# Larger slot distances in a slot-scheduled attention and MLP kernel: loads, q/k transposes, result stores

## The chip, the cores and the metric

One core of a Trainium2 chip. The metric is the device time of one execution, in microseconds (us). A profiled execution shows a span about 1.7 us shorter than the time of its run; numbers from a trace are compared with numbers from a trace only. The profiled execution of the kernel before took 338.71 us, 2 us less than the median of 340.72.

Engines: PE multiplies matrices, DVE is the vector engine, ACT the activation engine, POOL issues the casting loads, SP issues the transposes by DMA and the stores. "SPq" in a profile line is SP's queue.

## The reference, cut to what matters

```python
# B, H, S, D = 4, 8, 768, 64; chunks of 32 keys
k_min, k_max = min and max of k over each chunk
ub = sum_d max(q * k_min, q * k_max)             # a bound per query and chunk
top_chunks = the 6 chunks of largest ub, causal
attn = softmax(where(mask, q @ k.T / sqrt(D), -1e9)) @ v
x = attn, heads merged                           # 3072 x 512
out = softplus(x @ w_in) @ w_out                 # 512 -> 2048 -> 512
```

## The kernel before

The work is cut into 12 blocks of 256 query rows (block n), and time into "slots": one slot is one pair of score tiles (two score matmuls and their exponential on ACT, so 192 slots and 192 score exps). A block has 8, 16 or 24 slots. Other work is hung onto slot numbers: `at(slot, generator)` runs a piece of the preparation of a later block, `later` is a list of things that become due at a slot, and each slot also advances the MLP of earlier blocks by one step.

```python
    def turn_dma(nm, n, pool):                   # q or k transposed by DMA, issued on SP
        x_sb = loaded.pop((nm, n))
        xt = pool.tile([128, NT, NP, 128], BF16, name=nm + "t")
        nc.sync.dma_start_transpose(out=..., in_=...)
        turned[nm, n] = xt

    def prep_block(n):                           # all of this on DVE, except the two marked
        kt = turned.pop(("k", n))
        ...
        for t in range(NT):
            nc.vector.tensor_reduce(kx[:, 0, t], kc, axis=AX.X, op=ALU.max)   # kxf <- kt
            nc.vector.tensor_reduce(kx[:, 1, t], kc, axis=AX.X, op=ALU.min)
            yield
        put_extremes(...)                        # bd <- kxf
        qt = turned.pop(("q", n))
        nc.vector.tensor_scalar_max(qpos, qt, 0.0)
        yield
        ... qneg, qa
        for t in range(NT):
            bounds(...)                          # PE: ub <- bd, qpos, qneg; DVE: ub_sb, 8 largest
            choose(...)                          # mraw
            yield
        nc.sync.dma_start_transpose(out=mt, in_=mraw)     # SP
        ... ka, kb <- kt
        put_mask(n, mt, 0, 2)                    # qa, qt <- mt

    def ot_step(n, g, o_sb):                     # attention result turned to x, on SP
        nc.sync.dma_start_transpose(out=X[n]..., in_=o_sb...)
        if g == 1:
            ready[n] = clock[0] + 4              # the MLP of block n may start

    def y_gen(n):
        for u in range(NT):
            y = ps_y.tile(...)                   # ONE buffer in PSUM
            for f in range(KFF):
                nc.tensor.matmul(y, g[...], w_out_sb[...])
                ...
                        nc.vector.tensor_copy(y_sb, y)
                        nc.sync.dma_start(out=out[r0:r0 + 128, :], in_=y_sb)
```

SP and POOL issue in the order in which the code emits their work, from start to end. DVE, PE and ACT do so only for block 0; from block 1 on, the framework's scheduler picks their order when the program is built, from its own estimate of when each operand will be there. Once built, DVE works through its list in order, and an instruction that waits holds up all behind it: all 615 DVE instructions ran in the order of the built list.

The softmax here doesn't subtract the row's maximum and nothing guards it: scores larger than these inputs give would overflow.

## Time and profile before

| | kernel before |
|---|---|
| time, median of 3 runs | 340.72 us |
| span of the profiled run | 337.0 us |
| first score exp of block 2 | 79.7 us |
| last score exp | 307.2 us |
| from there to the end ("tail", MLP only) | 29.8 us |

I call the time between these two score exps the stream: 79.7 to 307.2 us, 227.5 us. What comes before it is the start, what comes after it the tail. The page of the kernel before, its span, PE's busy share, granted clock in tenths over 40 slices, and the chain that ended last by engine:

```profile
span 337.0 us, 6388 instructions
...
PE 261.4 (78%) x2411; PEld 185.2 (55%) x2440; DVE 168.5 (50%) x615; ACT 197.2 (59%) x350; POOL 115.7 (34%) x191
...
PEclk9999999856997999969999979789999799999999
...
PE 43%; DVE 23%; DMA 20%; ACT 4%; SPq 3%; POOL 3%; issue 2%; ACTq 0%
```

No engine is full, PE is the nearest, and its clock dips again and again. The list of waits of the same kernel (who waited for whom: us in total, times, longest):

```profile
DVE kxf L289 <- DMA kt<-k_sb: 30.1, 9, 7.8
...
PE y L415 <- DVE y_sb L420: 17.2, 7, 6.0
...
PE ub L201 <- DVE qpos L298: 10.1, 5, 2.9
...
DVE qa L279 <- DMA mt<-mraw_115: 8.3, 5, 2.7
...
DVE qa L279 <- DMA mt<-mraw_114: 7.7, 4, 3.3
```

How such waits reach PE is seen in the timeline of the kernel before around its longest stop in the stream (start, duration, engine, line, operation, output<-input; in brackets the idle time before and what ended it):

```profile
204.22 1.19 SPq L381 DMA_TRANSPOSE x<-o_sb  x1
...
205.51 1.25 SPq L166 DMA_TRANSPOSE kt<-k_sb  x1
...
212.00 0.69 DVE L289 TENSOR_REDUCE kxf<-kt 128x16 bf16<-128x512 bf16 x1 [7.81 <-DMA kt<-k_sb]
...
216.85 0.68 DVE L420 COPY y_sb<-y 128x512 f32<-128x512 f32 x1
...
217.58 1.86 PE L415 MATMUL y<-w_out_sb,g 128*128 128x512 bf16 x4 [6.02 <-DVE y_sb L420]
```

SP issues kt only at 205.5 us; DVE has kxf next in its list and stands for 7.8 us; the y_sb copy behind it is late; y has one PSUM buffer, so PE stands for 6.0 us. Then PE runs at half clock, as the table of windows shows (window and its length, then busy us of PE, PEld (PE's weight loads), DVE, ACT and POOL with the number of instructions, then clock, DMA share, GB/s):

```profile
211.50:217.60 6.10, 0.08 (x3) 0.02 (x1) 5.51 (x16) 0.70 (x2) 2.16 (x3) 0.77 1.11 86
217.60:221.30 3.70, 3.70 (x14) 1.99 (x14) 0.99 (x3) 0.60 (x1) 0.00 (x0) 0.50 0.37 106
221.30:224.00 2.70, 2.70 (x28) 1.96 (x27) 0.00 (x0) 2.39 (x5) 1.24 (x2) 0.95 0.00 0
```

In the stream the PE stops of 0.4 us and more add up to 24.6 us, and the clock stands at half for 25.9 us (about 13 us lost, if PE had work all that time).

The row of a DMA on its issuing engine is only its issue: kt takes 1.25 us on SP and lands a median of 4.7 us after its issue began. The Trainium skill ("Perfetto Trace Analysis", section "Per-instruction lifecycle") says that on DMAs the entire data movement falls outside the profiled window; this trace agrees.

### The profile page before, as it was taken

To read this page: it belongs to the slowest core of one execution; us is meant where nothing else is said; L and a number is where in the kernel's file an instruction comes from. 1 tells how busy PE (TensorE), PEld (TensorE's weight loads), DVE (VectorE), ACT (ScalarE), POOL (GpSimd) and SP (SyncE) were. 2 spreads that over 40 slices of the span, in tenths; PEclk is the share of its full clock that TensorE was granted. 3 is DMA by queue.
4 is the path that set the end of the run, shared out by engine and by line. 5 is a ranking of instruction groups with operands and counts; after the bars stand their busy time and mean duration, and the time that the engine had idled before them with its cause. 6 is when DMAs were issued, how large, how long until landed. Compare 5 with 4: busy or idle time off the path is not lost.

```text
span 337.0 us, 6388 instructions
## 1 busy us (share of the span) xinstructions
PE 261.4 (78%) x2411; PEld 185.2 (55%) x2440; DVE 168.5 (50%) x615; ACT 197.2 (59%) x350; POOL 115.7 (34%) x191
## 2 busy tenths in 40 slices
PE   1234579428978879589899699299898799999994
PEld 0122447124665567457575587167665677776561
DVE  5877700287687565616854652737454932112001
ACT  3333359104893479547774869168764798886180
POOL 8334796422542633412445404213431110100000
PEclk9999999856997999969999979789999799999999
DMA  9929999996995992946966949937946211011101
GB/s 173 206 43 162 106 182 178 148 84 127 86 153 43 131 135 52 109 64 108 82 79 114 170 46 81 107 35 125 108 67 111 65 31 49 33 39 40 47 33 62
DMA packets 121374, 32.14 MB, mean 95 GB/s; under 512 B 115200, under 2 KB 117760, under 8 KB 121344
## 3 DMA queue, kind: packets, MB, share of 16 engines
q0 software_dynamic: 67168, 12.33, 48.9%
q1 hardware_dynamic: 51024, 18.62, 28.3%
q10 hardware_dynamic: 3152, 0.79, 1.4%
q8 instruction: 19, 0.31, 0.4%
q14 instruction: 11, 0.09, 0.1%
HBM read 27.26 MB, written 6.29 MB: 100 GB/s over the span
## 4 chain that ended last, share of the span: by engine, by line
PE 43%; DVE 23%; DMA 20%; ACT 4%; SPq 3%; POOL 3%; issue 2%; ACTq 0%
PE y L415 19%; PE hp L402 13%; DMA kt<-k_sb 10%; PE o_ps L363 4%; PE s_ps L338 3%; DVE y_sb L420 3%; DMA q_sb<-in_q_dram 3%; DMA two<-in_k_dram 3%; DVE kxf L290 3%; DVE kxf L289 3%; PE s_ps L340 2%; DMA x<-o_sb 2%; DVE bd_112 L191 2%; DMA qt<-q_sb 2%; DVE qpos L298 1%
## 5 line engine op out<-in xcount | busy, mean ns | idle before, releaser
L342 ACT ACTIVATE pt<-s_ps 128x512 bf16<-128x512 f32 (+1 forms) x192 | 103.3, 550 | 85.3 <-PE s_ps L340 85.2
L402 PE MATMUL hp<-x,w_in_sb 128*128 128x256 bf16 x768 | 107.1, 283 | 11.9 <-DMA x<-o_sb 11.1
L415 PE MATMUL y<-w_out_sb,g 128*128 128x512 bf16 x355 | 96.9, 395 | 19.1 <-DVE y_sb L420 17.2
L346 POOL TENSOR_SCALAR_AFFINE_SELECT pt<-pt 128x256 bf16<-128x256 bf16 x96 | 39.7, 415 | 174.6 <-ACT pt L342 174.4
L402 PEld LDWEIGHTS <-w_in_sb 128*128 128x128 bf16 x768 | 74.6, 101 | 23.8 <-issue 11.8
L404 ACT ACTIVATE e_sb<-hp 128x512 f32<-128x512 f32 x96 | 57.8, 605 | 31.7 <-PE hp L402 31.6
L415 PEld LDWEIGHTS <-g 128*128 128x128 bf16 x384 | 35.8, 100 | 48.7 <-issue 22.8
L406 ACT ACTIVATE g<-e_sb 128x1024 bf16<-128x1024 f32 x48 | 51.2, 1067 | 0.2
L420 DVE COPY y_sb<-y 128x512 f32<-128x512 f32 x24 | 16.5, 688 | 38.2 <-PE y L415 38.0
L363 PEld LDWEIGHTS <-pt 128*128 128x128 bf16 x672 | 32.0, 102 | 4.8 <-issue 0.6
L369 DVE RECIPROCAL rec<-o_ps 128x4 f32<-128x4 f32 x48 | 8.6, 179 | 48.8 <-PE o_ps L363 48.4
L289 DVE TENSOR_REDUCE kxf<-kt 128x16 bf16<-128x512 bf16 x20 | 13.6, 680 | 30.2 <-DMA kt<-k_sb 30.1
L373 DVE TENSOR_TENSOR o_sb<-o_ps,rec 128x256 bf16<-128x256 f32 x48 | 20.2, 422 | 1.4 <-DVE rec L369 0.3
L113 POOL DMA_DIRECT2D k_sb<-in_k_dram x20 | 17.8, 894 | 8.4 <-DMA kt<-k_sb 4.8
L363 PE MATMUL o_ps<-v_106,pt 128*128 128x65 bf16 x336 | 20.2, 202 | 0.1
L113 POOL DMA_DIRECT2D q_sb<-in_q_dram x20 | 18.0, 904 | 1.9 <-DMA qt<-q_sb 1.3
L363 PE MATMUL o_ps<-v_107,pt 128*128 128x65 bf16 x336 | 16.3, 195 | 0.8 <-DVE o_sb L373 0.8
L203 DVE TENSOR_TENSOR ub_sb<-ub,cmask 128x192 f32<-128x192 f32 x20 | 7.0, 352 | 16.7 <-PE ub L202 16.7
L338 PE MATMUL s_ps<-qa,ka_108 96*128 96x256 bf16 x48 | 14.8, 309 | 0.6 <-ACT pt L342 0.4
L338 PE MATMUL s_ps<-qt,kb_110 128*128 128x256 bf16 x48 | 14.9, 311 | 0.4 <-ACT pt L342 0.3
L279 DVE COPY qa<-mt 32x512 bf16<-32x512 bf16 x20 | 6.7, 333 | 16.4 <-DMA mt<-mraw_115 8.3
L338 PE MATMUL s_ps<-qt,kb_111 128*128 128x256 bf16 x48 | 13.5, 281 | 0.0
(147 smaller groups left out, 309.2 us busy)
## 6 DMA issues: line engine op xcount, KB each, us to landing
out_dram<-y_sb SPq DMA_DIRECT2D x24, 256.0 KB, 2.2
k_sb<-in_k_dram POOLq DMA_DIRECT2D x20, 128.0 KB, 4.7
q_sb<-in_q_dram POOLq DMA_DIRECT2D x20, 128.0 KB, 5.3
w_in_sb<-in_moe_w_in_dram POOLq DMA_DIRECT2D x4, 512.0 KB, 5.6
w_out_sb<-in_moe_w_out_dram POOLq DMA_DIRECT2D x4, 512.0 KB, 7.7
v_107<-in_v_dram POOLq DMA_DIRECT2D x12, 128.0 KB, 4.9
v_106<-in_v_dram POOLq DMA_DIRECT2D x10, 128.0 KB, 4.2
two<-in_k_dram SPq DMA_DIRECT2D x6, 128.0 KB, 6.2
```

The source lines that it names most:

```text
L113: nc.gpsimd.dma_start(out=xb[:, t], in_=rows(nm, n, t))
L289: nc.vector.tensor_reduce(kx[:, 0, t], kc, axis=AX.X, op=ALU.max)
L338: nc.tensor.matmul(s_ps[:, 0:QB], kk[0:nr, p, j * 128:(j + 1) * 128], qq[0:nr, :, p, :], start=True, stop=True)
L342: nc.scalar.activation(pt[:, h, j:j + 2].rearrange("k j c -> k (j c)")[:, 0:w], s_ps[:, 0:w], ACT.Exp, scale=scale)
L346: nc.gpsimd.affine_select(out=diag, in_=diag, compare_op=ALU.is_ge, fill=0.0, base=0, channel_multiplier=-1, pattern=[[0, 2], [1, 128]])
L363: nc.tensor.matmul(o_ps[:, u, h], pt[:, h, j, c0:c0 + 128], V[b % 2][:, j, 2 * p + h, :], start=(j == 0), stop=(j == t0 + u))
L373: nc.vector.tensor_tensor(o_sb[:, :, p % 2], o_ps[:, :, :, 0:D], rec.to_broadcast([128, NT, 2, D]), op=ALU.mult)
L402: nc.tensor.matmul(hp[:, fi], w_in_sb[:, dt, ft * 128:(ft + 1) * 128], X[n][:, dt // 2, :, dt % 2, :], start=(dt == 0), stop=(dt == KDM - 1))
L404: nc.scalar.activation(e_sb[:, f2 * 2:f2 * 2 + 2], hp, ACT.Exp)
L406: nc.scalar.activation(g[:, f4 * 4:(f4 + 1) * 4], e_sb, ACT.Ln, bias=1.0)
L415: nc.tensor.matmul(y, g[:, f, u * 128:(u + 1) * 128], w_out_sb[:, f, :], start=(f == 0), stop=(f == KFF - 1))
L420: nc.vector.tensor_copy(y_sb, y)
```

## The change

The intent is to take waits away by distance: data asked for earlier, and stores issued only when their data is surely there, so that the in-order SP queue is not held up.

```diff
-            later.append((clock[0] + 2, 0.0, ot_step, (n, p // 2, O.pop((n, p // 2)))))
+            later.append((clock[0] + 4, 0.0, ot_step, (n, p // 2, O.pop((n, p // 2)))))
...
-            ready[n] = clock[0] + 4
+            ready[n] = clock[0] + 6
...
-                        nc.sync.dma_start(out=out[r0:r0 + 128, :], in_=y_sb)
+                        if clock[0] == NEVER:
+                            store(r0, y_sb)
+                        else:
+                            later.append((clock[0] + 3, 0.0, store, (r0, y_sb)))
...
-        if n == 2:
-            base = 17
+        base = {2: 17, 3: 32}.get(n, base)
...
-            at(base - PER - 6, later_loads(n))
+            at(base - PER - 10, later_loads(n))
...
-        at(base - (4 if n > 2 else 1), turns)
-        at(base - (3 if n > 2 else 1), turns)
+        at(base - (12 if n > 2 else 1), turns)
+        at(base - (9 if n > 2 else 1), turns)
```

So there are three parts: loads and q/k transposes earlier, with block 3's preparation moved from slot 26 to 32 ("turns"), stores later ("stores"), x transposes and the MLP start later ("x delay").

More of the change, by code (lines that the diff above doesn't have):

```diff
@@ L407, in h_gen, with store @@
                 yield
+    def store(r0, y_sb):
+        nc.sync.dma_start(out=out[r0:r0 + 128, :], in_=y_sb)
     def y_gen(n):
```

## The prediction

> **What bounds it now.** No engine is full: the page gives PE 78% of 337.0 us, ACT 59%, DVE 50%. PE is the limit wherever nothing stalls: in the table of windows it is busy 25.8 of 26 us at 284-310, clock 1.00. Elsewhere it stops. From 76 to 310 us it is busy 204.9 of 234 us. The timeline of PE names the stops over 0.5 us: y matmuls waiting for the y_sb copy on DVE (4.5, 1.6, 6.0, 0.8 us), ub matmuls waiting for qpos on DVE (2.9, 2.1, 2.8, 1.9), one x transpose (1.4); about 24 us. After most of the longer ones the clock reads 0.50 to 0.59 for some 3.7 us (144.3-148.0: 0.50), about 1.8 us lost each, 8 us in all. The Trainium skill ("TensorE: Matmul & The Clock Gate", Part 1) says an idle window of about 3.4 us halves the clock; this trace agrees roughly (also after 1.9 us).
>
> DVE is late because it is in order and sits on kxf until the kt transpose lands: 30.1 us in 9 waits (list of waits), 9.9% of the chain. kt is late because the SP queue is in order too: it stands behind result stores and mask transposes whose data DVE has not made (64 and 44 us of SP waits for y_sb), then takes 4.7 us to land.
>
> **What changes.** No arithmetic, no bytes. In SP's built order kt of the next block moves ahead of the mask transpose mt; qt comes right behind mt; stores fall back three slots. Loads go 4 slots earlier. x transposes come 2 slots later and the MLP starts 4 slots later: by counting slots, 4 MLP steps (about 0.9 us each) move into the tail, roughly neutral because PE is full there.
>
> **How much is won.** Not all 32 us. DVE and PE order is chosen by the scheduler, and the built DVE order shows it also hoists kxf and qpos: often right behind what releases their transpose. So DVE still stops on kt (two in three blocks of a period, 4 to 6 us), and newly on qt: mt and qt are issued back to back (1.2 us each), mt lands in 2.4, qt in 5.1, with 1.2 us of mask copies between, so some 2.5 us a block. But qpos is then ready long before its ub matmuls, so the ub stops go, and the y stops shrink. Walking one period of three blocks (72 us) with trace durations I get PE stops of about 1, 2, and 3 to 4 us (y and o_ps matmuls waiting for DVE evacuations), about 6.5 us plus perhaps 2 us of slow clock, against 12 and 3.5 now: 7 us a period, 3.3 periods in the stream. The start to 79 us is bound by loads and stays, within 2 us.
>
> **Prediction: 319 us** (-21), range 308 to 333. Faster by over 2%: 0.86; within 2%: 0.12; slower: 0.02.
>
> **Signs.** Stops of ub for qpos nearly gone; y_sb stops under 3 us each; clock over 76-310 us above 0.95; kxf waits for kt from 30 to about 20 us; new qpos waits for qt of 10 to 18 us; SP waits on y_sb well under 64 us; tail after the last score 3 to 4 us longer; PE busy time about unchanged or less (warmer clock).
>
> **What would make it wrong.** If the hoisted kxf/qpos block o_sb and y_sb evacuations longer than I walked (each 6 us stop passing wholly to PE), the gain falls to a few us. If transposes land faster in an emptier queue, DVE never stops and 305 is possible. If block 5's earlier loads slow the crowded start, up to 4 us come back.

## The result, and the profile after

The changed kernel takes 330.86 us (330.64 to 331.73, 3 runs) against 340.72: ratio 0.9729, 95% interval 0.9679 to 0.9779. A ratio here is the mean time of one kernel's runs over that of the other's runs of the same rounds, so not quite the ratio of the quoted medians. Executions over 1.5% slower than the fastest of the same kernel are left out of the means. The direction was right and the time lay in the range, but the gain was 9.9 us where 21.7 were forecast (340.72 to 319).

The page after:

```profile
span 329.1 us, 6389 instructions
...
PE 256.9 (78%) x2409; PEld 183.7 (56%) x2440; DVE 163.4 (50%) x615; ACT 197.0 (60%) x350; POOL 117.2 (36%) x191
...
PEclk9999999965897899999979999999799999999998
...
PE 33%; DMA 27%; DVE 25%; ACT 6%; issue 3%; SPq 3%; POOL 2%; ACTq 0%; POOLq 0%
```

PE's matmul share is 78% in both, though the time differs by 2.7%. The Trainium skill ("Perfetto Trace Analysis", section "Identifying the Most-Contended Engine") calls matmul busy % no good measure of how near PE is to its roofline, and proposes MFU (the share of peak FLOP/s) and the busy share of LDWEIGHTS (PE's weight loads). No run here computes MFU, and the share of weight loads moved only from 55% to 56%, so neither share by itself shows the gain.

The list of waits after:

```profile
DVE kxf L289 <- DMA kt<-k_sb: 34.3, 8, 7.2
...
DVE qa L279 <- DMA mt<-mraw_115: 13.8, 5, 3.9
PE y L418 <- DVE y_sb L423: 11.4, 7, 3.6
...
DVE qa L279 <- DMA mt<-mraw_114: 10.6, 4, 3.3
...
PE ub L201 <- DVE qpos L298: 7.4, 1, 7.4
PE ub L201 <- DVE ub_sb L203: 6.9, 3, 5.6
```

The transposes stand 9 to 12 slots ahead in the code instead of 3 or 4, and DVE waits for kt not less but more: 34.3 us, where it was 30.1. (The one wait of ub for qpos, 7.4 us, lies at 70 us, before the stream.) The timeline after, around the longest such wait of DVE in the stream:

```profile
224.17 0.42 DVE L373 TENSOR_TENSOR o_sb<-o_ps,rec 128x256 bf16<-128x256 f32 x1
...
224.62 1.19 SPq L381 DMA_TRANSPOSE x<-o_sb  x1
...
225.91 1.25 SPq L166 DMA_TRANSPOSE kt<-k_sb  x1
...
231.79 0.69 DVE L289 TENSOR_REDUCE kxf<-kt 128x16 bf16<-128x512 bf16 x1 [7.20 <-DMA kt<-k_sb]
...
235.05 0.69 DVE L423 COPY y_sb<-y 128x512 f32<-128x512 f32 x1
...
235.79 1.44 PE L418 MATMUL y<-w_out_sb,g 128*128 128x512 bf16 x3 [3.55 <-DVE y_sb L423]
```

The same picture as before: DVE goes from the o_sb evacuation straight to kxf, and SP can issue kt only after the x transpose that this o_sb releases. The built order of DVE says why; this is the place of one such kxf, that of block 8, in the lists of the changed kernel (engine, number in its list without waits and branches, line, operation, operands; from the built program, not from the profile):

```
DVE 363  L373 TensorTensor  o_sb_2052<-o_ps_2129,rec_2161
DVE 364  L289 TensorReduce  kxf_2559<-kt_2318
SP   51  L381 DmaTransposeAnt  x_2221<-o_sb_2052
SP   52  L166 DmaTransposeAnt  kt_2318<-k_sb_2010
```

The code emits this kxf twelve slots after its kt; the scheduler has pulled it up to right behind the instruction that sets the transpose off. The distance in the code is twelve slots, that in DVE's list is nothing.

How far each kernel has come at the start of a given score exp (us from the start of the span, from the timeline of ACT):

| score exp number | before | after | difference |
|---|---|---|---|
| 25th (block 2) | 79.7 | 79.3 | -0.4 |
| 57th (block 4) | 114.2 | 117.4 | +3.2 |
| 105th (block 7) | 184.3 | 181.7 | -2.6 |
| 153rd (block 10) | 257.0 | 249.3 | -7.7 |
| 192nd, the last | 307.2 | 296.5 | -10.7 |
| end of span | 337.0 | 329.1 | -7.9 |

The first lap is 3.6 us slower (from -0.4 to +3.2), the others gain 5.8, 5.1 and 3.0 us, and 2.8 us are given back in the tail, which grows from 29.8 to 32.7 us (rounded from the trace).

### The profile page after: what moved, and what is told of

It is laid out like the page before. It is cut to its first block, busy times and chain, and to the rows that moved or that the text cites. A ratio compares the mean times of both kernels' runs of the same rounds, so it can differ in the third digit from the quotient of the medians.

```text
span 329.1 us, 6389 instructions
## 1 busy us (share of the span) xinstructions
PE 256.9 (78%) x2409; PEld 183.7 (56%) x2440; DVE 163.4 (50%) x615; ACT 197.0 (60%) x350; POOL 117.2 (36%) x191
## 4 chain that ended last, share of the span: by engine, by line
PE 33%; DMA 27%; DVE 25%; ACT 6%; issue 3%; SPq 3%; POOL 2%; ACTq 0%; POOLq 0%
PE y L418 16%; DMA kt<-k_sb 12%; PE hp L402 9%; DMA k_sb<-in_k_dram 5%; DMA two<-in_k_dram 3%; PE s_ps L338 3%; DVE y_sb L423 3%; DMA mt<-mraw_115 3%; DVE kxf L290 2%; DMA mt<-mraw_114 2%; PE s_ps L340 2%; PE o_ps L363 2%; DVE kxf L289 2%; DVE o_sb L373 2%; ACT g L406 2%
## 5 line engine op out<-in xcount | busy, mean ns | idle before, releaser
L418 PE MATMUL y<-w_out_sb,g 128*128 128x512 bf16 x353 | 93.5, 386 | 13.6 <-DVE y_sb L423 11.4
L346 POOL TENSOR_SCALAR_AFFINE_SELECT pt<-pt 128x256 bf16<-128x256 bf16 x96 | 40.5, 423 | 161.5 <-ACT pt L342 161.4
L402 PEld LDWEIGHTS <-w_in_sb 128*128 128x128 bf16 x768 | 73.8, 100 | 17.1 <-issue 5.1
L404 ACT ACTIVATE e_sb<-hp 128x512 f32<-128x512 f32 x96 | 58.5, 613 | 24.4 <-PE hp L402 24.1
L418 PEld LDWEIGHTS <-g 128*128 128x128 bf16 x384 | 35.1, 98 | 41.6 <-issue 14.7
L423 DVE COPY y_sb<-y 128x512 f32<-128x512 f32 x24 | 16.5, 687 | 42.6 <-PE y L418 42.5
L289 DVE TENSOR_REDUCE kxf<-kt 128x16 bf16<-128x512 bf16 x20 | 13.6, 678 | 34.3 <-DMA kt<-k_sb 34.3
L363 PE MATMUL o_ps<-v_106,pt 128*128 128x65 bf16 x336 | 19.5, 201 | 1.7 <-DVE o_sb L373 1.6
L113 POOL DMA_DIRECT2D q_sb<-in_q_dram x20 | 18.7, 937 | 2.5 <-DMA qt<-q_sb 1.3
L363 PE MATMUL o_ps<-v_107,pt 128*128 128x65 bf16 x336 | 15.9, 193 | 0.8 <-DVE o_sb L373 0.8
L338 PE MATMUL s_ps<-qa,ka_108 96*128 96x256 bf16 x48 | 15.5, 324 | 0.5 <-ACT pt L342 0.5
L338 PE MATMUL s_ps<-qt,kb_110 128*128 128x256 bf16 x48 | 14.7, 306 | 0.5 <-ACT pt L342 0.3
L340 PE MATMUL s_ps<-qa,ka_108 96*128 96x128 bf16 (+1 forms) x48 | 13.9, 289 | 0.0
L338 PE MATMUL s_ps<-qa,ka_109 96*128 96x256 bf16 x48 | 13.5, 281 | 0.0
```

Of the source, the lines that this page charges most:

```text
L113: nc.gpsimd.dma_start(out=xb[:, t], in_=rows(nm, n, t))
L338: nc.tensor.matmul(s_ps[:, 0:QB], kk[0:nr, p, j * 128:(j + 1) * 128], qq[0:nr, :, p, :], start=True, stop=True)
L340: nc.tensor.matmul(s_ps[:, QB:w], kk[0:nr, p, (j + 1) * 128:(j + 2) * 128], qq[0:nr, 1 if last else 0:, p, :], start=True, stop=True)
L346: nc.gpsimd.affine_select(out=diag, in_=diag, compare_op=ALU.is_ge, fill=0.0, base=0, channel_multiplier=-1, pattern=[[0, 2], [1, 128]])
L363: nc.tensor.matmul(o_ps[:, u, h], pt[:, h, j, c0:c0 + 128], V[b % 2][:, j, 2 * p + h, :], start=(j == 0), stop=(j == t0 + u))
L402: nc.tensor.matmul(hp[:, fi], w_in_sb[:, dt, ft * 128:(ft + 1) * 128], X[n][:, dt // 2, :, dt % 2, :], start=(dt == 0), stop=(dt == KDM - 1))
```

## The experiments

Theory: what was won is small because the scheduler hoists the DVE readers of the transposes (kxf, qpos, and their companions) up to the transposes, so the new distance never reaches DVE. Rival one: the transposes themselves come too late, in the in-order SP queue or the crowded DMA, and the order of DVE does not matter. Rival two: another part of the change (stores, x delay) carries the gain, or spoils it. All experiments gave correct results. Each batch ran beside the kernel before on one chip (7 runs of it, medians 339.03, 341.00 and 340.06 us, one slow run in the last). The x delay alone was not run.

The table holds all runs; times are medians of the fast executions, of two only for early_as_before (their mean); "stops" are PE's idle stretches of 0.4 us or more within the stream (25th to 192nd score exp), "half" the time within it at a clock of 0.5, both from the profiled run. "kxf" is DVE's total wait of kxf for kt from the list of waits.

| run | time, us | ratio (95%) | stream | tail | stops | half | kxf |
|---|---|---|---|---|---|---|---|
| before | 340.72 | 1 | 227.5 | 29.8 | 24.6 | 25.9 | 30.1 |
| after | 330.86 | 0.973 (0.968 to 0.978) | 217.2 | 32.7 | 18.9 | 19.3 | 34.3 |
| turn_only | 331.29 | 0.973 (0.963 to 0.982) | 220.3 | 29.8 | 24.9 | 10.2 | 42.4 |
| store_only | 328.93 | 0.970 (0.961 to 0.978) | 217.6 | 29.4 | 17.5 | 19.2 | 35.1 |
| no_x_delay | 329.41 | 0.972 (0.965 to 0.980) | 218.7 | 29.4 | 22.0 | 10.2 | 40.9 |
| early_as_before | 331.51 | 0.974 (0.967 to 0.981) | 217.6 | 32.6 | 20.2 | 18.7 | 33.2 |
| dve_order | 313.26 | 0.924 (0.919 to 0.929) | 200.7 | 32.6 | 6.8 | 12.2 | 10.6 |
| before_dve_order | 316.60 | 0.934 (0.928 to 0.939) | 207.0 | 29.8 | 8.3 | 15.9 | 18.8 |
| pin_turned | 314.33 | 0.925 (0.919 to 0.930) | 199.8 | 32.7 | 7.9 | 3.6 | 6.1 |
| before_pin_turned | 320.60 | 0.942 (0.937 to 0.947) | 208.3 | 29.8 | 11.9 | 11.4 | 13.4 |
| dve_order_turn_only | 309.53 | 0.911 (0.901 to 0.922) | 201.1 | 29.8 | 3.9 | 9.3 | 10.5 |
| dve_order_no_x_delay | 307.28 | 0.908 (0.901 to 0.915) | 197.5 | 29.4 | 2.9 | 4.0 | 9.8 |

### dve_order and before_dve_order: DVE in the order of the code

```diff
-    consts(1)
-    run_block(1, 0.8)
-    ...
+    with tc.manual_schedule(engines={ET.DVE}):
+        consts(1)
+        run_block(1, 0.8)
+        ...
```

Only the order of DVE is fixed; PE and ACT stay with the scheduler, which moves some of their work in answer (588 of PE's 4880 instructions changed place in the built list, by 2.5 places in the mean over all). Once on the changed kernel, once on the kernel before.

> Changed kernel, with DVE kept in program order from block 1 on, so that kxf and qpos stand where their slot puts them, 12 and 11 slots behind their transposes. If the scheduler's hoisting eats the new distance (my theory): waits of kxf for kt fall from 34 us to under 10 us, PE stops over 0.5 us between 76 and 310 us from about 24 us to under 12 us, time 316 to 325 us. If the transposes themselves come late on the in-order SP queue or the crowded DMA (rival): the waits stay above 25 us and the time at 327 to 334 us.

> Kernel before, with DVE in program order in the same way. Theory: the distance of 4 slots is too short whatever the order, kxf waits for kt stay at 15 to 30 us, time 332 to 342 us. Rival (the order of DVE alone is worth the gain, the distances nothing): as fast as the changed kernel with DVE in order, within 3 us.

The changed kernel drops to 313.26 us, further than the theory's 316 to 325; the waits for kt fall to 10.6 us, a hair above the 10 it allowed. The waits for kt and for y_sb in dve_order, from its list of waits:

```profile
DVE kxf L289 <- DMA kt<-k_sb: 10.6, 1, 10.6
...
PE y L418 <- DVE y_sb L423: 1.1, 2, 0.8
```

The one wait for kt left is that of block 2, at the start, whose transpose is issued one slot ahead in all versions. PE stops in the stream fall to 6.8 us. Rival one falls: SP issues the same transposes in the same order (its sequence in the two traces is the same), and the waits are gone.

The second run did not do what I expected. The kernel before, with DVE in the order of the code, takes 316.60 us, where I expected 332 to 342; kxf still waits 18.8 us (10.3 of it at the start), inside my 15 to 30. The other 8.5 us lie in the stream, and part of them reaches PE: four ub stops for qpos, 6.6 us together, come 4 to 5 us behind such waits. So 4 slots are a little short, but my belief that they are too short whatever the order is wrong in size: the two kernels with DVE in order differ by 3.3 us (the rival had said within 3), the two with the scheduler's order by 9.9, and the order alone is worth 22 us to the kernel before, more than twice the whole change.

### pin_turned and before_pin_turned: only the readers of the transposes held

Program order moves all of DVE's work. To see whether the readers of the transposes alone matter, those were queued behind the evacuation that was emitted last before their slot (order of issue only, no wait on data):

```diff
+        evac[0] = nc.vector.tensor_tensor(o_sb[:, :, p % 2], ...)     # likewise at y_sb
...
+            with tc.issue_after(evac[0].ins):
                 nc.vector.tensor_reduce(kx[:, 0, t], kc, axis=AX.X, op=ALU.max)
                 nc.vector.tensor_reduce(kx[:, 1, t], kc, axis=AX.X, op=ALU.min)
...                      # the same around qpos, around qneg and qa, around ka, around kb
```

> Changed kernel with only the DVE readers of the q and k transposes (kxf, qpos, qneg, qa, ka, kb copies) held behind the evacuation emitted last before their slot; all other DVE order is the scheduler's. Theory (hoisting of these readers is what eats the distance): 311 to 317 us like the run with DVE in order, kxf waits for kt under 15 us. Rival (DVE in order won by other moves, of masks, bounds or y_sb): 322 to 331 us.

> Kernel before with the same hold. It got 316.6 us with all of DVE in order. Theory (the readers of the transposes alone): 314 to 322 us, with 15 to 25 us of kxf waits, since 4 slots are short. Rival (other moves): 328 to 340 us.

Both came out where the theory put them: 314.33 and 320.60 us. The line of kt in pin_turned, and that of PE:

```profile
DVE kxf L291 <- DMA kt<-k_sb: 6.1, 1, 6.1
...
PE y L424 <- DVE y_sb L429: 5.5, 5, 3.0
```

Holding back six kinds of DVE instruction in five places, and nothing else, gives within about 1 us what DVE in full program order gives the changed kernel, and in the kernel before most of it (ratio 0.942 against 0.934). The scheduler was free to move other work when they were held, but in before_pin_turned it did not: PE's weight loads, ACT, POOL and SP run through the same sequence in its trace as in that of the kernel before, and the built lists of PE agree too. Only DVE's order differs, and the time falls by 20 us. The hoisting of these readers, as a group, is shown to be the cost, in both kernels; which of the six counts most was not tried. Where they are held, the whole change is worth 6 us (320.60 to 314.33); in before_pin_turned kxf still waits 13.4 us for kt, less than the 15 to 25 us I expected:

```profile
DVE kxf L291 <- DMA kt<-k_sb: 13.4, 5, 7.0
```

### turn_only, store_only, no_x_delay: the parts of the change

turn_only leaves out the later stores and the x delay; store_only has only the stores; no_x_delay leaves out only this:

```diff
-            later.append((clock[0] + 4, 0.0, ot_step, ...))
+            later.append((clock[0] + 2, 0.0, ot_step, ...))
-            ready[n] = clock[0] + 6
+            ready[n] = clock[0] + 4
```

> Only loads and q/k transposes earlier; stores and x transposes as before. Theory: this part carries the gain of the stream and costs no tail: 327 to 332 us. Rival (the later stores clear the SP queue, and that is the gain): 335 to 341 us.

> Kernel before with only the stores three slots behind. Theory: kt still stands behind the mask transpose on SP, its readers are hoisted, so 335 to 341 us. Rival (clearing SP of stores that wait for y_sb is the gain): 328 to 334 us.

> Changed kernel with x transposes and the MLP start at the old 2 and 4 slots. Theory: the later MLP start costs about 3 us of tail and some of the early stop of PE for x at 78 us (5.8 us), so 325 to 329 us, tail after the last score exp back from 32.6 to about 30 us. Rival (the x delay is what lets kt pass on SP): 331 to 336 us.

The turns alone give 331.29 us, as expected. The stores alone give 328.93 us, and here the rival was right: I expected no gain. Each of the two yields about the whole gain, and together they yield no more; why they do not add up is open. The traces show different ways. With the stores alone the ub stops for qpos shrink (9.8 to 2.4 us in the stream), the long y stops stay. With the turns alone the sum of stops does not change (24.6 and 24.9 us) and kxf waits most of all (42.4 us), but the time at half clock falls from 25.9 to 10.2 us: it has one stop over 3 us in the stream, the kernel before has two, of 4.5 and 6.0 us. That many small stops cost less clock than a few long ones is read from these two traces alone; which stop halves the clock I can not say in each case.

Taking the x delay out gave 329.41 us, a hair above my 325 to 329, and the same ratio as the whole change (0.972 and 0.973). The tail is back to 29.4 us, and the stream is longer by 1.5 us. So with the scheduler's order the delay does no measurable good or harm.

### early_as_before: block 3 as before

The slow first lap (25th to 57th exp) suggested that block 3's move did harm: its preparation at slot 32 and its kt ahead of block 2's mask.

```diff
-        base = {2: 17, 3: 32}.get(n, base)
+        if n == 2:
+            base = 17
...                      # and for n = 3 the transposes 4 and 3 slots ahead
```

> Changed kernel, with block 3 as before (preparation at slot 26, its transposes 4 and 3 slots ahead). Theory: the move of block 3's kt ahead of the mask of block 2, and of its preparation to slot 32, makes the start slow, so the 56th score exp comes back from 117.4 to about 114.5 us and the total is 326 to 329 us. Rival (the earlier loads or the later x do it): 56th exp stays at 116 to 118 us, total 330 to 333 us.

That theory fell. The 57th exp (the expectation counts from zero and calls it the 56th) came at 115.6 us, between what the two expected, the last exp at 296.5 us as in the changed kernel, and two executions took 330.85 and 332.17 us, as the rival said. The trace of the changed kernel says better what slows the lap: at 104.2 us PE stands 5.6 us for ub_sb, because DVE waited for block 3's mask (2.4 us) and then, in front of ub_sb, for the kt of block 5:

```profile
95.03 1.45 SPq L166 DMA_TRANSPOSE kt<-k_sb  x1
...
96.07 0.28 DVE L279 COPY qa<-mt 32x512 bf16<-32x512 bf16 x1 [2.37 <-DMA mt<-mraw_115]
...
100.67 0.69 DVE L289 TENSOR_REDUCE kxf<-kt 128x16 bf16<-128x512 bf16 x1 [2.69 <-DMA kt<-k_sb]
...
103.78 0.34 DVE L203 TENSOR_TENSOR ub_sb<-ub,cmask 128x192 f32<-128x192 f32 x1
...
104.17 0.20 PE L201 MATMUL ub<-bd_113,qpos 128*128 128x48 bf16 x1 [5.63 <-DVE ub_sb L203]
```

The same stop is in turn_only (5.9 us) and no_x_delay (5.8 us), and it is in neither store_only nor pin_turned. So it goes both without the earlier turns and without the hoisted reader.

### dve_order_no_x_delay and dve_order_turn_only: what beats both

These combine DVE in order with the whole change less the x delay, and with the turns alone.

> Changed kernel, DVE in program order, x transposes and MLP start at the old 2 and 4 slots. Theory (PE is full both in the stream and in the tail, so 4 MLP steps cost the same in either): within 2 us of 313 us, the tail after the last score exp shorter by about 3 us and the stream longer by as much. Rival (the shorter tail is a gain of its own): 309 to 311 us.

> Only loads and q/k transposes earlier, DVE in program order. Theory (with the readers in place the transposes' distance is what is left of the change): 312 to 315 us, like the whole change with DVE in order. Rival (the stores give the last 3 us): 316 to 318 us, like the kernel before with DVE in order.

The first is the fastest of all, 307.28 us, 9.2% under the kernel before and 6 us under dve_order; I had expected no difference, and even the rival's 309 to 311 was too high. Its page shows what PE looks like without stops (busy tenths and clock over the 40 slices):

```profile
PE   0333369914799879999999999999999999999984
...
PEclk9999996975599999999999999999999999999999
```

Where the 6 us come from: in dve_order the x transposes come later and the MLP starts later, so PE has less to do in the gap around 75 to 85 us. There it stands 4.8 us for the mask copies of block 2 and 2.3 us for an x; without the delay these are 1.7 and 2.0 us. First two lines dve_order, last two dve_order_no_x_delay:

```profile
77.73 0.37 PE L338 MATMUL s_ps<-qa,ka 96*128 96x256 bf16 x1 [4.77 <-DVE qa L279]
...
83.98 0.58 PE L402 MATMUL hp<-x,w_in_sb 128*128 128x256 bf16 x2 [2.30 <-DMA x<-o_sb]
...
75.28 1.01 PE L402 MATMUL hp<-x,w_in_sb 128*128 128x256 bf16 x4 [2.04 <-DMA x<-o_sb]
...
78.00 0.37 PE L338 MATMUL s_ps<-qa,ka 96*128 96x256 bf16 x1 [1.71 <-DVE qa L279]
```

The half-clock time falls from 12.2 to 4.0 us, and at the 57th exp the kernel is 5.4 us ahead. Work was moved from a place where PE waits to the tail, where it is full. With the turns alone it takes 309.53 us, under both expectations (312 to 315 us, and the rival's 316 to 318); whether the stores add anything to that is left open (0.911 without and 0.908 with them, intervals overlapping).

A rough check of the accounting: take the change in stops, half the change in time at half clock, and, where the x delay is in, 3.6 us of MLP work that leaves the stream (4 steps of about 0.9 us). For turn_only that gives -7.5 us of stream, measured -7.2; store_only -10.4 and -9.9; the changed kernel -12.6 and -10.4; before_dve_order -21.3 and -20.5; dve_order -28.3 and -26.9. It errs by up to 4 us, always on the high side, but it orders the runs as measured in size, except two that lie 0.4 us apart (dve_order and dve_order_turn_only). It is an estimate from the traces behind the table above.

## Why the prediction was right or wrong

- **What bounds the kernel: right.** PE stops for DVE, DVE for transposes, and the lost clock besides; once these are gone (dve_order_no_x_delay) the stream shrinks from 227.5 to 197.5 us.
- **The mechanism that limits the change: right.** The prediction said that the scheduler hoists kxf and qpos to right behind what releases their transpose, so that DVE still stops. dve_order and pin_turned show it: with these readers held, the gain is 26.7 us instead of 9.9. The run before_pin_turned, where only DVE's order differs, shows it without any other change.
- **The size: wrong. The step that failed is "about 6.5 us plus perhaps 2 us of slow clock, against 12 and 3.5 now: 7 us a period, 3.3 periods in the stream".** The "after" side held: 18.9 us of stops in 167 slots, that is 3.5 periods of 48 slots, 5.4 us a period where 6.5 were walked. The "now" side fits the worst period, multiplied (the stretch of 72 us from 99 us on has 12.5 us of stops): 12 us times 3.3 is 40 us, and the same text had read "about 24 us" for all stops. The trace of before has 24.6 us, 7.0 a period. So the stops fell by 5.7 us and not by 18. From the prediction's own totals, 24 and 8 us now against 3.3 times 6.5 and 2 later, the gain would have been about 4 us, nearer to the measured 9.9 than 21 is. The clock gave less than forecast too, but by little: from 25.9 to 19.3 us at half, about 3.3 us, against 3.3 times 1.5, some 5 us. Over 3.5 periods, a period measured 7.0 and 3.7 us (stops and slow clock) before, 5.4 and 2.8 after: 2.6 us won, where 7 were forecast.
- **kxf waits "from 30 to about 20 us": wrong,** they rose to 34.3 us. **New waits of qpos for qt of 10 to 18 us: wrong,** 1.2 us. The mask transpose lands later than assumed (median 4.0 us after issue instead of 2.4) and DVE waits there instead: 24.4 us for mt, after 16.0.
- **ub stops for qpos nearly gone: right in the stream** (9.8 us to none over 0.4 us), but 6.1 us for ub_sb came in their place. **y stops under 3 us: nearly,** two are longer, 3.1 and 3.6. **Clock above 0.95 over 76-310 us: just,** 0.95 after 0.94. **PE busy time about unchanged or less: right,** 256.9 us after 261.4.
- **The start, within 2 us: right up to 79 us; but the next lap lost 3.6 us.** The prediction named a loss of up to 4 us there as a risk, but from block 5's earlier loads; the trace shows block 5's kt held behind an x transpose on SP, and its hoisted reader in front of ub_sb.
- **Tail 3 to 4 us longer: nearly** (2.9), and **"roughly neutral"**: right under the scheduler's order (no_x_delay); with DVE in order, which the prediction did not speak of, the delay costs 6 us.
- **SP waits on y_sb well under 64 us: right** (46.7 us for the stores; 43.9 with the stores alone, which win as much as everything). How much of the gain goes through these waits is open.

## What to carry to other kernels

A distance in the code is worth only what is left of it in the built order of the reading engine: before lengthening prefetch distances, look up where the readers stand in that engine's list, and hold them back if a scheduler pulls them forward to the transfer. When forecasting, take the "now" from the sum over the whole trace and check it against the stop list, never from one stretch times a count. And don't move work out of a stretch where the busiest engine waits into one where it is full.

## What the Trainium skill lacked or had wrong

- "TensorE: Matmul & The Clock Gate", Part 1, gives about 3.4 us of idleness before the clock halves. In the kernel before, a stop of 1.9 us at 265.5 us was followed by a mean clock of 0.57 over the next 3.5 us, while one of 2.1 us at 124.4 us was followed by 1.00. The length fits otherwise: the stretches at half clock wholly within the stream are 3.41 or 6.83 us long.
- The pages on DMA give bandwidths for transposes by DMA, but none gives the time from issue to landing: a 128 x 1024 bf16 one takes about 1.25 us to issue on SP and lands a median of 4.7 us (kt) and 5.1 us (qt) after its issue began, 5.4 and 3.8 us in the changed kernel; the smaller mask transpose 2.4 and 4.0 us.
- None of the pages on profiles warns that a build-time scheduler may move the readers of a transfer up to it: here it cost 16.5 us of 330.9 in the changed kernel (314.33 us with the readers held), and nothing in a list of waits tells it from a late transfer.
